# Two-way attention and a squared-ReLU layer on one core: transposes moved from TensorE to DMA, a new order at the start, two column softmaxes moved to the end

## The chip, the core and the metric

The kernel runs on one core of one Trainium2 chip. Its engines work through queues of their own and meet at semaphores: TensorE (PE; its weight loads are listed as PEld), VectorE (DVE), ScalarE (ACT), GpSimd (POOL) and SyncE (SP, which only issues DMAs here). Sixteen DMA engines move data for all of them. TensorE writes to PSUM, eight banks of 2 KB in each of 128 partitions; VectorE and ScalarE copy from there to SBUF. The metric is the device time of one execution in microseconds, as the median of several runs.

## The reference

There are 8 batches of 8 heads, each with a sequence x of 512 rows and a state of 32 rows, both 64 wide. Attention goes both ways over the same scores, and all 4352 rows of the result go through a two-layer network (512 to 2048 to 512):

```python
scores = scale * x @ state.T                    # 512 x 32 per head
xread  = softmax(scores, over the 32) @ state
sread  = softmax(scores.T, over the 512) @ x    # 32 x 512
X = concat(xread, sread), heads side by side    # (8 * 544) x 512
out = (s * relu(X @ w_in) ** 2 + b) @ w_out
```

## The kernel before

Matmuls are in fp16 with fp32 sums. For the 512 x-rows of a batch `X @ w_in` is never formed with xread: the kernel makes M = state @ w_in for each head (8 heads x 32 state rows = two groups of 128 rows, by 2048 columns), and the first layer is A @ M, where A is the first softmax. The names, with lines of the profile:

- **stT**: the transposed state, 64 rows of a head on 64 partitions. `turn_states` makes eight TensorE transposes of the cast states (line 84 through 78), `build_stT` eight ScalarE copies (line 175).
- **xT**: transposed x. `at_x` does 16 TensorE transposes of 128x128 (tile `xps`) and two ScalarE copies of 1024 columns a batch (line 205).
- **T**: the scores, 8 matmuls of 512 columns on 64x32 tiles of the array (`at_T`, line 215), into two banks.
- **First softmax, over 32**: VectorE transposes T in 32x32 blocks (U, 225), takes a maximum per block (mu, 229) and subtracts it (Dm, 235); ScalarE takes the exponential (E1, 242); VectorE sums (z and rz, 249 and 250), multiplies (At, 254) and transposes back (A, 261).
- **Second softmax, over 512 (column softmax)**: VectorE takes the maximum of T (nm, nms: 267, 273), ScalarE the exponential with its sum (E2, 278), VectorE multiplies by the reciprocal (q, a2: 285, 287). `at_aps` transposes a2 with 8 TensorE transposes and one ScalarE copy (a2T, 296), `at_V` multiplies by x with 32 small matmuls (tile `vps`), and VectorE copies the result to srdT (315).
- **M**: four units of 512 columns a batch, each of 8 matmuls (tile `mps`) and two ScalarE copies (330).
- **First layer**: for each f of 16, two matmuls of 512 columns (tile `hps`, 338), an eviction with ReLU on ScalarE to r (340) and a square on VectorE to g (345). **Second layer**: 16 output units a batch of 4 matmuls (tile `ops`, 361), four of them to one block of 128 rows, which VectorE scales and shifts (osb, 371) and SP stores.

The order of the work is written out by hand: what is called first stands first in each engine's queue. A `phase` is sixteen steps. In phase n step f is the first layer of batch n, f, and one unit of the second layer of batch n-1. Lists of (step, piece) hang the other pieces in: in phase n the scores and softmaxes of batch n+1, its a2T and V, and four units of M. Phase 0 and phase 1 have lists of their own, since the start is behind; the last phase, `sr`, runs the first layer of all 256 state rows beside the second layer of batch 7, and the second layer of the state rows follows as a tail.

```python
for b in range(1, B):
    before = []
    if b + 2 < B:
        before += plan_xread(b + 2, (0, 1, 2, 3, 4, 5, 5, 6, 7, 9, 10, 11))
        before += plan_sread(b + 2, (7, 8, 11))
```

SP loads all states (one DMA of 512 KB) and x of batch 0 in fp32 (four of 256 KB), and ScalarE and VectorE cast them. GpSimd's queue loads with a cast to fp16, in this order: w_in 0, x 1, w_in 1 to 3, w_out 0 to 3, x 2; the later x when a buffer is free. One x is four DMAs, in runs of 64 elements.

PSUM is shared out in pairs of banks: `ps_t` for T; `ps_a` (two single banks) for transposes, V and M; `ps_h` for the first layer; `ps_o` for the second.

Of the kernel before, what the change touches and what calls it, by code (L numbers as in the profile page):

```python
# [10 lines left out]
FP32 = mybir.dt.float32  # L11
# [4 lines left out]
def kernel(  # L16
# [11 lines left out]

# [9 lines left out]
    P = 128  # L41
# [6 lines left out]
    ST = S + Ns  # L48
    scale = float(1.0 / np.sqrt(D))
# [3 lines left out]
    konst = ctx.enter_context(tc.tile_pool(name="konst", bufs=1))  # L53
    wpool = ctx.enter_context(tc.tile_pool(name="wpool", bufs=1))
    stage = ctx.enter_context(tc.tile_pool(name="stage", bufs=1))
# [8 lines left out]
    ps_a = ctx.enter_context(tc.tile_pool(name="ps_a", bufs=2, space=bass.MemoryType.PSUM))  # L64
# [4 lines left out]
    def bank(shape, dtype, name, pool=None, tag="pa"):  # L69

        full = (pool or ps_a).tile([P, 2048 // mybir.dt.size(dtype)], dtype, name=name, tag=tag)
        names = " ".join("abc"[: len(shape) - 1])
        sizes = dict(zip("abc", shape[1:]))
        return full[:, 0 : int(np.prod(shape[1:]))].rearrange(f"p ({names}) -> p {names}", **sizes)
# [8 lines left out]
    def transp(out, in_, identity):  # L83
        return mm(out, in_, identity, tp=(0, 0), is_transpose=True)

    RP = B * H * Ns // P
    ident16 = konst.tile([P, P], FP16, name="ident16")
    ident_dr = nc.inline_tensor(np.eye(P, dtype=np.float16), name="ident_const")  # L90
    xf = stage.tile([P, H, SCH, D], FP32, name="xf")
    stf = stage.tile([P, RP, D], FP32, name="stf")
    stn = konst.tile([P, RP, D], FP16, name="stn")
    s_bc = konst.tile([P, 1], FP32, name="s_bc")
    b_bc = konst.tile([P, 1], FP32, name="b_bc")
    ones16 = konst.tile([P, P], FP16, name="ones16")
    bias_bc = konst.tile([P, DM], FP32, name="bias_bc")
    srdT = konst.tile([P, NK, Ns, B], FP16, name="srdT")
    stT = konst.tile([P, B * NK, Ns], FP16, name="stT")
    w_in16 = [wpool.tile([P, NK, 512], FP16, name=f"w_in16_{j}") for j in range(NJ)]  # L100
    w_out16 = [wpool.tile([P, 4, DM], FP16, name=f"w_out16_{q}") for q in range(NKF // 4)]
    xn_t = {}

    def new_xn(b):
        xn_t[b] = xpool.tile([P, SCH, H, D], FP16, name=f"xn_{b}", tag="xn")
        return xn_t[b]

    def load_x(b, c):
        xn = new_xn(b) if c == 0 else xn_t[b]
        nc.gpsimd.dma_start(out=xn[:, c], in_=x[b].rearrange("h (q c) d -> c q h d", q=P)[c])  # L110
# [6 lines left out]
    def load_w_out(q):  # L117
# [4 lines left out]
    nc.sync.dma_start(  # L122
        stf,
        state.rearrange("b h n d -> (b h n) d").rearrange("(p r) d -> p r d", r=RP),
    )
    nc.scalar.dma_start(ident16, ident_dr.ap())
    for k in range(NK):
        nc.sync.dma_start(
            xf[:, 2 * k : 2 * k + 2].rearrange("q h c d -> q h (c d)"),
            x[0, 2 * k : 2 * k + 2].rearrange("h (q c) d -> q h (c d)", q=P),  # L130
        )
# [3 lines left out]
    nc.vector.tensor_copy(stn[:, : RP // 2], stf[:, : RP // 2])  # L135
    nc.gpsimd.tensor_copy(stn[:, RP // 2 :], stf[:, RP // 2 :])
    load_w_in(0)
    for c in range(SCH):
        load_x(1, c)
    for j in range(1, NJ):  # L140
        load_w_in(j)
    for q in range(NKF // 4):
        load_w_out(q)
    for c in range(SCH):
        load_x(2, c)
# [8 lines left out]


# [4 lines left out]
    def heads():  # L160
        for hp in range(4):
            for g in range(NG):
                h = 4 * g + (hp ^ g)
                yield h // 2, h % 2, g, hp

    def build_stT(sl, copies):
        if "sps" not in at[0]:
            turn_states()  # L170
        src = at[0]["sps"].rearrange("p r (bk m u) -> p m bk u r", m=2, u=2)
        dst = stT.rearrange("p bk (u r o) -> p o bk u r", u=2, o=2)
        for m in range(2):
            for o in range(2):
                copies[m](dst[D * m : D * m + D, o, sl], src[D * o : D * o + D, m, sl])

    def turn_states():
        sps = at[0]["sps"] = bank([P, RP // 2, P], FP16, "sps", ps_h, "ph")
        for r in range(0, RP, 2):
            transp(sps[:, r // 2, :], stn[:, r : r + 2, :], ident16)  # L180
# [4 lines left out]
    def sm(b, key, shape, dtype, pool=None, bufs=None):  # L185
        t = (pool or smpool).tile(shape, dtype, name=f"{key}_{b}", tag=key, bufs=bufs)
        at[b][key] = t
        return t

    def blocks(t):  # L190
        return t.rearrange("p g (j n) -> p (g j) n", n=32)

    def over_n(t):
        return t.unsqueeze(2).to_broadcast([P, t.shape[1], 32])

    def at_x(b, kk, copy, n=2):

        if kk == 0:
            sm(b, "xT", [P, NK, S], FP16, apool)
        xps = bank([P, n, S], FP16, f"xps_{b}_{kk}")  # L200
        for k in range(n):
            for c in range(SCH):
                h = 2 * (n * kk + k)
                transp(xps[:, k, P * c : P * c + P], xn_t[b][:, c, h : h + 2, :], ident16)
        copy(at[b]["xT"][:, n * kk : n * kk + n, :], xps)  # L205

    def at_T(b):
        if b:
            T = at[b]["T"] = ps_t.tile([P, NG, S], FP32, name=f"T_{b}", tag="pt")
        else:  # L210
            T = [bank([P, S], FP32, f"T_{b}_{g}", ps_o, "po") for g in range(NG)]
        Tg = at[b]["Tg"] = [T[:, g, :] if b else T[g] for g in range(NG)]
        xT = at[b]["xT"]
        for k, m, g, hp in heads():
            mm(
                Tg[g][Ns * hp : Ns * hp + Ns, :],
                stT[D * m : D * m + D, NK * b + k, :],
                xT[D * m : D * m + D, k, :],
                tp=(D * m, Ns * hp),
            )  # L220


    def at_U(b, g):
        U = sm(b, "U", [P, NG, S], FP32) if g == 0 else at[b]["U"]
        nc.vector.transpose(U[:, g, :], at[b]["Tg"][g])  # L225

    def at_mu(b, g0, g1):
        mu = sm(b, "mu", [P, NG * NSB], FP32) if g0 == 0 else at[b]["mu"]
        nc.vector.tensor_reduce(  # L229
            mu[:, NSB * g0 : NSB * g1], blocks(at[b]["U"][:, g0:g1, :]), AX.X, ALU.max  # L230
        )

    def at_D(b, g0, g1, eng):
        Dm = sm(b, "Dm", [P, NG, S], FP32) if g0 == 0 else at[b]["Dm"]
        eng.tensor_tensor(  # L235
            blocks(Dm[:, g0:g1, :]), blocks(at[b]["U"][:, g0:g1, :]),
            over_n(at[b]["mu"][:, NSB * g0 : NSB * g1]), ALU.subtract,
        )

    def at_E1(b, g0, g1):  # L240
        E1 = sm(b, "E1", [P, NG, S], FP16) if g0 == 0 else at[b]["E1"]
        nc.scalar.activation(E1[:, g0:g1, :], at[b]["Dm"][:, g0:g1, :], AF.Exp, scale=scale)

    def at_z(b, g0, g1):

        z = sm(b, "z", [P, NG * NSB], FP32) if g0 == 0 else at[b]["z"]
        rz = sm(b, "rz", [P, NG * NSB], FP32) if g0 == 0 else at[b]["rz"]
        sl = slice(NSB * g0, NSB * g1)
        nc.vector.tensor_reduce(z[:, sl], blocks(at[b]["E1"][:, g0:g1, :]), AX.X, ALU.add)
        nc.vector.reciprocal(rz[:, sl], z[:, sl])  # L250

    def at_At(b, g0, g1, eng):
        At = sm(b, "At", [P, NG, S], FP16) if g0 == 0 else at[b]["At"]
        eng.tensor_tensor(  # L254
            blocks(At[:, g0:g1, :]), blocks(at[b]["E1"][:, g0:g1, :]),
            over_n(at[b]["rz"][:, NSB * g0 : NSB * g1]), ALU.mult,
        )

    def at_A(b, g0, g1):
        A = sm(b, "A", [P, NG, S], FP16, apool, 3) if g0 == 0 else at[b]["A"]  # L260
        nc.vector.transpose(A[:, g0:g1, :], at[b]["At"][:, g0:g1, :])  # L261


    def at_nm(b):
        nm, nms = sm(b, "nm", [P, NG], FP32), sm(b, "nms", [P, NG], FP32)
        if b:
            nc.vector.tensor_reduce(nm, at[b]["T"], AX.X, ALU.max, negate=True)
        else:
            for g in range(NG):
                nc.vector.tensor_reduce(  # L270
                    nm[:, g : g + 1], at[b]["Tg"][g], AX.X, ALU.max, negate=True
                )
        nc.vector.tensor_scalar(nms, nm, scale, None, ALU.mult)  # L273

    def at_E2(b):
        E2, rs = sm(b, "E2", [P, NG, S], FP16), sm(b, "rs", [P, NG], FP32)
        for g in range(NG):
            nc.scalar.activation(  # L278
                E2[:, g, :], at[b]["Tg"][g], AF.Exp,
                bias=at[b]["nms"][:, g : g + 1], scale=scale, accum_out=rs[:, g : g + 1],  # L280
            )
# [8 lines left out]

    def at_aps(b):
        aps = bank([P, SCH, NG, P], FP16, f"aps_{b}")
        for g in range(NG):
            for c in range(SCH):
                transp(aps[:, c, g, :], at[b]["a2"][:, g, P * c : P * c + P], ident16)
        nc.scalar.copy(sm(b, "a2T", [P, SCH, NG, P], FP16, apool), aps)
# [16 lines left out]

    def at_srd(b):
        nc.vector.tensor_copy(srdT[:, :, :, b], at[b]["vps"])


    def at_M(b, j, pool=None, tag="pa"):
        if j == 0:
# [269 lines left out]
```

## Time and profile before

| | before |
|---|---|
| median of 3 runs | 249.57 us (249.25 to 249.7) |
| span of the profiled execution | 247.4 us |
| time of that execution beside its span | not given apart; the median lies 2.17 us above the span |
| mean granted TensorE clock | 0.993 |
| busy: PE, PEld, DVE, ACT, POOL | 224.2, 105.9, 160.2, 157.5, 31.7 us |
| ops (512 matmuls), hps (256) | 131.7, 78.0 us |
| xps (128 transposes), aps (64) | 11.9, 4.9 us |
| mps (256), T (64), vps (256) | 14.3, 4.9, 5.6 us |
| ACT: r, M, xT, a2T | 76.5, 34.4, 15.2, 8.1 us |

The spans of matmuls overlap, since they are pipelined: what one group costs is the distance from its start to the start of the next. In the chain of work that ended last TensorE has 81% of the span, VectorE 11%, ScalarE 4%. In a line of the order of time the two numbers in front are the start and the length in microseconds; the bracket at its end is the idle time before it and what ended it. Phases begin, by the first xps of a batch, at 42.15 (phase 1), 68.56 (phase 2) and 167.76 (phase 6); phase 7 ends at 214.62, with the first matmul of `sr`, and the tail begins at 235.58.

### The profile page before, as it was taken

Reading aid. Unit: us, or ns where it says so; the run is one execution under the profiler, and the core shown is the slowest. Engines: PE = TensorE matmul, PEld = TensorE weight load, DVE = VectorE, ACT = ScalarE, POOL = GpSimd, SP = SyncE. Lnnn points to the kernel's source line nnn. Section 1 sums busy time; section 2 is a strip of 40 time slices with the busy share of each in tenths; the row PEclk is TensorE's granted clock in tenths of the full one; section 3 lists DMA queues with packets and bytes.
Section 4 is the critical chain, followed back from the end, with each engine's and each line's share of the span. In section 5 each row is a group of like instructions: output and inputs, shape, how many; then the busy total and the mean of one; then the engine's idle time right before and its main releaser. Section 6 shows DMA issues by size and latency. Waiting matters only on the chain.

```text
span 247.4 us, 4277 instructions
## 1 busy us (share of the span) xinstructions
PE 224.2 (91%) x1673; PEld 105.9 (43%) x1673; DVE 160.2 (65%) x306; ACT 157.5 (64%) x284; POOL 31.7 (13%) x41
## 2 busy tenths in 40 slices
PE   1549499968999999999999999999999999999993
PEld 1222134534444444444544444444444444555652
DVE  0499965598659955995599549954996344433330
ACT  2766976768778757875787578757875655433200
POOL 3963100055040050005000000000000000000000
PEclk9999889999999999999999999999999999999999
DMA  5999990299592194119511111111111111121113
GB/s 169 198 186 206 207 143 2 80 75 75 73 117 56 42 107 65 42 46 103 69 44 42 45 42 42 45 42 46 42 42 45 42 42 42 45 86 42 45 45 84
DMA packets 40068, 18.66 MB, mean 75 GB/s; under 512 B 30320, under 2 KB 35696, under 8 KB 40048
## 3 DMA queue, kind: packets, MB, share of 16 engines
q0 software_dynamic: 33344, 7.87, 33.8%
q1 hardware_dynamic: 6272, 10.49, 11.9%
q8 instruction: 13, 0.21, 0.4%
q10 hardware_dynamic: 432, 0.03, 0.1%
q14 instruction: 7, 0.06, 0.1%
HBM read 17.34 MB, written 8.91 MB: 106 GB/s over the span
## 4 chain that ended last, share of the span: by engine, by line
PE 81%; DVE 11%; ACT 4%; DMA 2%; issue 1%; ACTq 0%
PE ops L361 43%; PE hps L338 21%; PE mps L78 4%; PE xps L78 3%; PE hps_sr L338 3%; PE vps L78 2%; DVE U L225 2%; DVE mu L229 2%; DMA stf<-in_state_dram 2%; PE ops_sr L551 1%; PE ops_sr L361 1%; PE aps L78 1%; PE T L78 1%; ACT r L340 1%; DVE g L345 1%; DVE A L261 1%
## 5 line engine op out<-in xcount | busy, mean ns | idle before, releaser
L361 PE MATMUL ops<-w_out,g 128*128 128x512 f16 x512 | 131.7, 380 | 0.0
L340 ACT ACTIVATE r<-hps 128x512 f16<-128x512 f32 x128 | 76.5, 606 | 34.5 <-PE hps L338 33.8
L345 DVE TENSOR_TENSOR g<-r 128x512 f16<-128x512 f16 x128 | 54.5, 431 | 50.7 <-ACT r L340 50.5
L338 PE MATMUL hps<-A,M 128*128 128x512 f16 x256 | 78.0, 389 | 3.9 <-ACT r L340 3.8
L361 PEld LDWEIGHTS <-g 128*128 128x128 f16 x512 | 50.3, 98 | 57.8 <-issue 0.8
L330 ACT CAST M<-mps 128x512 f16<-128x512 f32 x64 | 34.4, 594 | 11.1 <-PE mps L78 10.2
L338 PEld LDWEIGHTS <-M 128*128 128x128 f16 x256 | 21.2, 99 | 31.1 <-issue 16.5
L110 POOL DMA_DIRECT2D xn<-in_x_dram x28 | 24.6, 895 | 77.2 <-PE vps L78 47.1
L371 DVE SCALAR_TENSOR_TENSOR osb<-ops,s_bc,bias_bc 128x512 f32<-128x512 f32 x32 | 23.9, 746 | 0.6 <-PE ops L361 0.6
L205 ACT COPY xT<-xps 128x1024 f16<-128x1024 f16 (+1 forms) x16 | 15.2, 959 | 8.2 <-PE xps L78 8.2
L78 PEld LDWEIGHTS <-xn 128*64 128x64 f16 (+1 forms) x384 | 14.5, 110 | 13.6 <-issue 4.6
L78 PE MATMUL mps<-w_in,stT 64*32 64x512 f16 x256 | 14.3, 399 | 2.9 <-DMA w_in<-in_moe_w_in_dram 1.6
L78 PE MATMUL xps<-ident,xn 128*128 128x128 f16 x128 | 11.9, 241 | 4.3 <-ACT xn L461 2.4
L340 ACT ACTIVATE r_sr<-hps_sr 128x256 f16<-128x256 f32 x16 | 6.1, 383 | 14.5 <-PE hps_sr L338 14.5
L345 DVE TENSOR_TENSOR g_sr<-r_sr 128x256 f16<-128x256 f16 x16 | 4.7, 292 | 12.4 <-ACT r_sr L340 12.1
L78 PEld LDWEIGHTS <-stT 64*32 64x32 f16 x320 | 4.5, 89 | 18.7 <-issue 18.6
L278 ACT ACTIVATE E<-T,nms 128x512 f16<-128x512 f32 x16 | 10.8, 688 | 1.1 <-DVE nms L273 1.1
L225 DVE STREAM_TRANSPOSE U<-T 128x512 f32<-128x512 f32 x16 | 10.5, 692 | 0.7 <-PE T L78 0.7
L261 DVE STREAM_TRANSPOSE A<-At 128x1024 f16<-128x1024 f16 (+1 forms) x9 | 10.1, 1120 | 0.1
L235 DVE TENSOR_TENSOR Dm<-U,mu 128x1024 f32<-128x1024 f32 (+1 forms) x9 | 9.9, 1100 | 0.1
L254 DVE TENSOR_TENSOR At<-E,rz 128x1024 f16<-128x1024 f16 (+1 forms) x9 | 9.9, 1096 | 0.1
L229 DVE TENSOR_REDUCE mu<-U 128x32 f32<-128x1024 f32 (+1 forms) x9 | 9.8, 1094 | 0.1
(44 smaller groups left out, 126.2 us busy)
## 6 DMA issues: line engine op xcount, KB each, us to landing
out_dram<-osb SPq DMA_DIRECT2D x32, 256.0 KB, 2.2
xn<-in_x_dram POOLq DMA_DIRECT2D x28, 128.0 KB, 5.3
w_in<-in_moe_w_in_dram POOLq DMA_DIRECT2D x4, 512.0 KB, 10.5
w_out<-in_moe_w_out_dram POOLq DMA_DIRECT2D x4, 512.0 KB, 15.7
xf<-in_x_dram SPq DMA_DIRECT2D x4, 256.0 KB, 5.8
stf<-in_state_dram SPq DMA_DIRECT2D x1, 512.0 KB, 3.7
out_dram<-osb_sr SPq DMA_DIRECT2D x1, 256.0 KB, 3.0
out_dram<-osb_sr SPq DMA_DIRECT2D x2, 128.0 KB, 2.3
```

Source lines behind the costliest of these rows:

```text
L78: return nc.tensor.matmul(out, lhsT, rhs, start=start, stop=stop, tile_position=tp, is_transpose=is_transpose, skip_group_check=skip,)
L110: nc.gpsimd.dma_start(out=xn[:, c], in_=x[b].rearrange("h (q c) d -> c q h d", q=P)[c])
L205: copy(at[b]["xT"][:, n * kk : n * kk + n, :], xps)
L225: nc.vector.transpose(U[:, g, :], at[b]["Tg"][g])
L229: nc.vector.tensor_reduce(mu[:, NSB * g0 : NSB * g1], blocks(at[b]["U"][:, g0:g1, :]), AX.X, ALU.max)
L261: nc.vector.transpose(A[:, g0:g1, :], at[b]["At"][:, g0:g1, :])
L330: nc.scalar.copy(at[b]["M"][:, g, 512 * j : 512 * j + 512], mps[g])
L338: nc.tensor.matmul(hps, lhsT, rhs, start=(i == 0), stop=(i == len(terms) - 1))
L340: nc.scalar.activation(r, hps, AF.Relu)
L345: nc.vector.tensor_mul(gt, r, r)
L361: nc.tensor.matmul(ops_t[tag, rr], G_t[tag][f][:, P * rr : P * rr + P], w_out_f(f), start=(f == 0), stop=(f == NKF - 1),)
L371: nc.vector.scalar_tensor_tensor(osb, ops_t.pop((tag, rr)), s_bc, bias_bc, ALU.mult, ALU.add)
```

## The change

- Three kinds of transpose go from TensorE and a copying engine to DMA transposes on SP's queue: states of batches 1 to 7 (`turn_states_dma`, 14 blocks of 128x128), x of batches 1 to 7 (`at_x_dma`, 16 blocks each) and a2 of all batches (in `at_a2`, 8 blocks). `at_aps`, `build_stT` and most uses of `at_x` go.
- States are loaded as rows (r p), two blocks first, and are cast twice side by side, so that a transposed block has each state on both halves of the partitions. A transposed block of x holds two neighbouring rows, one on each half of the partitions, so T's two banks are the two row parities p, with both head groups g in each: 16 matmuls of 256 columns.
- x of batch 0 is also loaded with a cast by GpSimd, first in its queue, in two halves; one x is one DMA (runs of 256 elements). The order is x 0, w_in 0, w_in 1, x 1, w_in 2, w_in 3, the casts of the states, w_out 0 to 3, x 2, x 3, x 4.
- The first softmax of batch 0 and the first layer's f 0 to 7 are done in halves (row parity p, head group g). Nine matmuls that compute nothing (`idle`) stand between them.
- M is made in pairs of units, one in `ps_a`, which is now one buffer of two banks, and one in `ps_t` (`own`); its copies hang in the four steps that follow.
- The column softmaxes of batches 0 and 1 are done in phase 7 (`late`), with their scores computed again; V of the others is one phase later.

```diff
-    nc.sync.dma_start(
-        stf,
-        state.rearrange("b h n d -> (b h n) d").rearrange("(p r) d -> p r d", r=RP),
-    )
+    state_rows = state.rearrange("b h n d -> (b h n) d").rearrange("(r p) d -> p r d", p=P)
+    nc.sync.dma_start(stf0[:, 0:2], state_rows[:, 0:2])
     nc.scalar.dma_start(ident16, ident_dr.ap())
-    for k in range(NK):
-        nc.sync.dma_start(
-            xf[:, 2 * k : 2 * k + 2].rearrange("q h c d -> q h (c d)"),
-            x[0, 2 * k : 2 * k + 2].rearrange("h (q c) d -> q h (c d)", q=P),
-        )
+    load_x(0, 2)
...
+    nc.sync.dma_start(stf1, state_rows[:, 2:])
     load_w_in(0)
-    for c in range(SCH):
-        load_x(1, c)
-    for j in range(1, NJ):
-        load_w_in(j)
+    load_w_in(1)
+    load_x(1)
+    load_w_in(2)
+    load_w_in(3)
+    for u in range(2):
+        nc.gpsimd.tensor_copy(stn[:, 2:, u], stf1)
     for q in range(NKF // 4):
         load_w_out(q)
-    for c in range(SCH):
-        load_x(2, c)
+    load_x(2)
...
+    def turn_states_dma(r0, r1):
+        nc.sync.dma_start_transpose(
+            stT[:, r0:r1], stn[:, r0:r1].rearrange("p r u d -> p (r u d)")
+        )
...
+    def at_x_dma(b):
+        new_xT(b)
+        nc.sync.dma_start_transpose(
+            at[b]["xT"], xn_t[b].rearrange("q h c d -> q (h c d)")
+        )
...
     def at_a2(b):
...
+        nc.sync.dma_start_transpose(
+            sm(b, "a2T", [P, NG * SCH, P], FP16, apool), a2.rearrange("p g s -> p (g s)")
+        )
...
+    def idle(n):
+        dps = ps_o.tile([P, DM], FP32, name=f"dps_{nc.next_id()}", tag="po")
+        for _ in range(n):
+            nc.tensor.matmul(dps, ones16[:, :P], ones16, start=True, stop=True)
...
+    turn_states(0, 2, act)
+    at_x(0, 0, (dve, act))
+    at_T(0, (0,))
+    idle(2)
+    for p in range(2):
+        at_U(0, p, 0)
+    at_mu(0, g=0)
+    at_D(0, g=0)
+    at_x(0, 1, (act, act))
+    at_T(0, (1,))
+    idle(1)
+    at_E1(0, g=0)
+    at_U(0, 0, 1)
...
+    at_M2(0, 0)
+    idle(4)
+    at_M2(0, 1)
+    idle(2)
+    turn_states_dma(2, RP)
+    at_x_dma(1)
+    at_x_dma(2)
...
+    for f in range(8):
+        layer1_x(0, f, 1)
+        square(0, f, 1)
+    at_M2(0, 2)
+    at_T(1)
+    for f in range(8, 12):
+        layer1_x(0, f)
...
+    at_M2(0, 3)
+    layer2(0, 0, 0)
...
+    at_M2(1, 0)
+    for q in (1, 2):
+        for rr in range(2):
+            layer2(0, rr, q)
+        at_M2(1, q, q == 2)
+    bias_sum()
+    for rr in range(2):
+        layer2(0, rr, 3)
+    bias_all()
+    for rr in range(2):
+        out_x(0, rr)
...
+    def late(b, s):
+        return [
+            (s[0], lambda: at_T(b)),
+            (s[1], lambda: at_nm(b)),
+            (s[2], lambda: at_E2(b, (0,))),
+            (s[3], lambda: at_E2(b, (1,))),
+            (s[4], lambda: at_a2(b)),
+            (s[5], lambda: at_V(b)),
+        ]
...
+    for b in range(0, B):
+        before, behind = [], l2(b) if b else first
+        behind = left + behind
+        if b + 3 < B:
+            before += [(0, lambda b=b: load_x(b + 3)), (9, lambda b=b: at_x_dma(b + 3))]
+        if b + 2 < B:
+            s = (0, 1, 2, 3, 4, 4, 5, 7, 8, 10, 11) if b else (4, 5, 6, 7, 8, 8, 9, 11, 12, 13, 15)
+            before += chain(b + 2, s)
+            before += [(13 if b else 15, lambda b=b: at_a2(b + 2))]
+        if b and b + 1 < B:
+            before += [(4, lambda b=b: at_V(b + 1))]
+        one = [(b + 1, 3), (b + 2, 0)][: B - 1 - b]
+        two = [(b + 2, 1), (b + 2, 2)] if b + 2 < B else []
+        make, copies, _ = pieces(7 if b else 9, 1, *one)
+        before, behind = before + make, behind + copies
+        make, copies, left = pieces(12 if b else 14, 0, *two)
+        before, behind = before + make, behind + copies
+        if b == B - 2:
+            before += late(0, (0, 1, 2, 3, 4, 11)) + late(1, (6, 7, 8, 9, 10, 14))
         phase(b + 1 if b + 1 < B else "sr", before, behind)
```

In `chain` the eleven steps are those of T, U, nm, E2 of each group, mu, Dm, E1, z, At and A.

## The prediction

> **What bounds the kernel now.** I read the page first (slices of the span, groups, DMA issues), then the busy time of stages cut where a batch's phase begins, then the order of time in the two stages that differ. The page says that TensorE is full from about 37 us to the end, and not before:
>
> ```profile
> PE   1549499968999999999999999999999999999993
> ...
> PEclk9999889999999999999999999999999999999999
> ```
>
> In the stages below (busy time by engine, granted clock, DMA share, GB/s; from 68.56 four whole phases) the steady phases are TensorE alone: 99.20 of 99.20 us, 24.80 each, with VectorE at 73.93 / 4 = 18.5 and ScalarE at 18.3. Phase 1 (42.15 to 68.56) is not: TensorE works 22.66 of 26.41.
>
> ```profile
> core 0: us, PE busy (x) PEld busy (x) DVE busy (x) ACT busy (x) POOL busy (x), PEclk, DMA share, GB/s
> ...
> 42.15:68.56 26.41, 22.66 (x242) 11.16 (x241) 19.47 (x39) 19.18 (x33) 7.96 (x10) 1.00 0.71 71
> 68.56:167.76 99.20, 99.20 (x770) 45.59 (x769) 73.93 (x137) 73.06 (x128) 9.58 (x11) 1.00 0.37 59
> 192.56:214.62 22.06, 22.06 (x122) 9.49 (x121) 9.45 (x21) 12.49 (x22) 0.00 (x0) 1.00 0.13 48
> ```
>
> TensorE in order of time (start, length, what): what a group takes is the distance to the next group, less 0.43 for two hps or 0.86 for four ops. Eight transposes take 0.44 (68.56 to 69.00). T and a unit of M back to back take 0.56; a unit alone 0.34; with the 0.09 of drain in front of each, 0.65 and 0.43.
>
> ```profile
> 68.56 0.61 PE L78 MATMUL xps<-ident,xn 128*128 128x128 f16 x8
> 69.00 0.59 PE L338 MATMUL hps<-A,M 128*128 128x512 f16 x2
> ...
> 72.13 0.41 PE L78 MATMUL T<-xT,stT 64*32 64x512 f16 x8
> 72.36 0.40 PE L78 MATMUL mps<-w_in,stT 64*32 64x512 f16 x8
> 72.69 0.61 PE L338 MATMUL hps<-A,M 128*128 128x512 f16 x2
> ...
> 76.68 0.41 PE L78 MATMUL mps<-w_in,stT 64*32 64x512 f16 x8
> 77.02 0.61 PE L338 MATMUL hps<-A,M 128*128 128x512 f16 x2
> ```
>
> At the start a chain sets the time: state, x, T at 10.57, softmax, first layer at 20.44. Beside it the cast loads run without a break until 36. GpSimd's waits for a landed w_in end at 19.52, 22.05 and 24.60, so a 512 KB slab lands every 2.55 us.
>
> ```profile
> 10.57 1.20 PE L78 MATMUL T<-xT,stT 64*32 64x512 f16 x8
> ...
> 20.44 3.81 PE L338 MATMUL hps<-A,M 128*128 128x512 f16 x10
> ...
> 24.60 0.87 POOL L110 DMA_DIRECT2D xn<-in_x_dram  x1 [1.67 <-DMA w_in<-in_moe_w_in_dram]
> ```
>
> The span is 247.4 us; no time of that execution is given beside it, so the sum goes against the median, 249.57, which holds 2.17 us around the span. I carry those unchanged.
>
> **Part 1, the steady phases 2 to 6.** Each loses 16 transposes of x and 8 of a2: 3 x 0.44 = 1.32 us of TensorE. M in pairs: today T + M (0.65) and three units alone (1.29) make 1.94; afterwards T (0.43) and two pairs (1.30) make 1.73, 0.21 less. T becomes 16 matmuls of 256 columns, the same columns: between 0 and 0.2 more (32 small vps matmuls issue in 0.64, 20 ns each, so 8 more cost at most 0.16). Net 1.3 to 1.5, taken 1.4: five phases, **-7.0**. Is all of it on the path? TensorE is busy throughout, and the next are VectorE (18.5, unchanged but for the form of nm and U) and ScalarE, which loses two xT copies and one a2T copy (1.01 each): 15.3. Both lie below 23.4. Four M copies now come on four steps with E1: 4 x (0.61 + 0.59) + 1.06 = 5.9 us against 4 steps of 1.29 and a pair of M, 5.8; two hps buffers cover that, and if not, a few tenths a phase.
>
> **Part 2, the DMA transposes.** Sixteen of them (one of 14 state blocks of 128x128, seven of 16 x blocks, eight of 8 a2 blocks) go on SP's queue, which after the first loads carries only stores today. No trace shows one. By rows:
>
> ```profile
> xn<-in_x_dram POOLq DMA_DIRECT2D x28, 128.0 KB, 5.3
> ...
> stf<-in_state_dram SPq DMA_DIRECT2D x1, 512.0 KB, 3.7
> ```
>
> Cheap end: 512 KB on the same queue, 3.7 us (stf); 256 KB stores land in 2.2. Dear end: the x loads in 256-byte pieces, 128 KB in 5.3 us, so 21.2 for the 512 KB of one x and 10.6 for an a2. I take 4 for x and 2.5 for a2, nearest to stf: the same queue and bytes, whole partitions. In a steady phase x is issued in step 9 and used in step 0 of the next, 7 steps or some 10 us later; a2 in step 13, used in step 4. Both are covered while x takes under about 10 us. They add waits: x 2's transpose holds SP until x 2 has landed near 37, with no store behind it before 40; a2's holds it for VectorE's two multiplications (0.7), with the phase's last store behind it; the stores have four osb buffers, a whole phase's worth, so neither costs. TensorE's T and V wait in order, and everything of TensorE stands behind them: that is where a late transpose would be paid. POOL goes from 28 x loads to 9, in 1 KB pieces; its 24.6 us of issue were hidden and nothing is gained there.
>
> **Part 3, the start, to the beginning of phase 2 (68.56 today).** The first state rows are 64 KB, x 0 comes as 512 KB in halves: first T near 6.3 against 10.57 (the x half reads 512 KB as stf does, 3.7 after an issue at 0.9; then 8 transposes and a copy, 1.03 + 0.6 in today's rows). Softmax of the first half: U 2 x 0.36, mu 0.69, Dm 0.69, the same for 256 more of the second group 1.1, E1 0.4, z 0.66 + 0.25, At 0.69, A 0.71, with the second x half between: 13.5. M 0 and 1 need w_in 1: slabs from 5.6 (x 0) at 2.55 each, and 2.2 for the other state rows, give 12; ScalarE has copied by 14.6. The second half's A follows near 18.2, first layer by 21.4 (16 evictions of 0.38). The nine idle matmuls (0.43 cold) lie in these waits; if the weights came early, four would delay M by 1.7. T of batch 1 needs GpSimd's state casts (2 x 1.5, after 9), their transpose and that of x 1, near 20 to 21: beside the path, by little. From 21.4 TensorE has 3.5 of hps, 1.7 of M, 6.9 of ops and 1.0 of cps, but w_out 3 lands only at 34 to 35.5 (eleven slabs and 1 MB of transposes at 2.55 per 512 KB). Then cps tail, 8 ops (1.73) and bias: phase 1 begins near 38.5, against 42.15, with one M unit and 8 ops more done.
> Phase 1 holds no x, a2T or V: TensorE 13.8 + T 0.43 + two pairs 1.3 = 15.5. It is VectorE's: x 2 lands at 37, its transpose at 42 to 43 (x 3 and x 4 load beside it), T at 43. Behind T stand U 1.38, nm 1.39, mu 1.21, Dm 1.22, ten squares 4.3, osb 0.75, z 1.56, At 1.21, A 1.24, a wait of 1.2 for E1: 15.5, and A of batch 2 is there at 59. So phase 2 begins at 59 instead of 68.56: **-9.6**. Two units of M are done ahead; three V are still owed.
>
> **Part 4, phase 7 and the end.** Phase 7 gains two T (0.86) and three V (3 x 0.64), loses two M units (0.86): **+1.9**. V of batch 1, in step 14, waits for an a2 whose E2 is in steps 8 and 9: 0 to 1 us, left in the range. The sr phase and the tail (32.8) stay.
> Sum: -7.0 - 9.6 + 1.9 = -14.7; 249.57 - 14.7 = **235** (234.9).
>
> A row that could take some of part 3 back: 24 to 36 us today has TensorE busy 8.77 of 12 and a granted clock of 0.86 (PEclk 8 in two slices); the hps at 29.88 take 1.87 for four, 0.47 each against 0.22, about 2.6 us over twelve matmuls. [...] It costs nothing while the weights set the pace, so my sum leaves it to the range.
>
> **Rivals.**
> *Transposes dear (ends slower).* At the dear end one phase needs 21.2 + 10.6 = 31.8 us of SP's queue against 23.4: five phases +42; the start has state (18.5), x 1, x 2 in a row from 12: x 2 at 73, A at 89, phase 2 thirty later than forecast: 235 + 72 = 307. It decides from 11.5 us per x: T of batch 2 then comes at 12 + 1.875 x 11.5 = 33.6, x 2 at 37 + 11.5 = 48.5 (6 later), and each steady phase waits 1.5 to 2 us (+8 to 9): all gain gone. Against it: nothing in the rows but stf and the stores; for it: the small-piece loads. [...]
> *The start gives little.* Transposes share the engines with loads (DMA share 1.5 from 12 to 36), so T 1, w_out 3 and x 2 slip by 4 to 9 us, each in front of an in-order TensorE: phase 2 at 63 to 68, total 239 to 244; 241 in the middle.
> *Steady phases do not shrink.* ScalarE's and VectorE's bunched steps hold them at 24.8: 235 + 7 = 242. For it: 5.9 against 5.8 above; against it: both engines under 19 in the sum.
>
> **How the numbers follow.** Forecast 0.56 (its own range 231 to 239), start gives little 0.18, no shrinking 0.10, transposes dear 0.14; 0.02 for a sum of losses that lands within 0.2% (0.5 us, about what can be told from no change). Faster 0.84, same 0.02, slower 0.14. The range, 230 to 246, leaves out the slower cases and a tail of the first.
>
> **What would show it.** Phase distance 23.4 (23.1 to 23.8) between first hps of successive batches; first hps near 14, phase 2 near 59, phase 7 near 24; SP's transposes landing in 3 to 5 us for x; no wait of T for xT after batch 2. Wrong if T waits for xT in each phase, if the relu of VectorE's late squares holds hps, or if w_out lands after 38.

## The result: slower, 258.75 us

The changed kernel takes 258.75 us (median of 4 runs, 258.57 to 259.38) against 249.41 us (249.13 to 249.7), a ratio of 1.0375 with a 95% interval of 1.0357 to 1.0393. The forecast was 235. The profiled execution took 258.57 us, with a span of 256.8. The slices of its page (each 6.4 us) say where:

```profile
PE   0796000499888999999999999999999999999993
...
PEclk9999655599999999999999999999999999999999
DMA  4999999940214476318814841183013132512113
```

Before, TensorE was never idle for a whole slice behind the first; now three slices hold nothing, with the granted clock down to half, while the DMA engines are full. TensorE in order of time shows the hole, and that it is one wait:

```profile
24.75 0.41 PE L74 MATMUL mps<-w_in,stT 64*32 64x512 f16 x8
48.50 0.63 PE L74 MATMUL T<-xT,stT 64*32 64x256 f16 x16 [23.34 <-DMA xT<-xn]
49.07 3.16 PE L358 MATMUL hps_None<-A,M 128*128 128x512 f16 x8
```

T of batch 1 waits 23.34 us for the transposed x of batch 1, and all of TensorE stands behind it. The chain that ended last, up to that T (start, length, what), tells what it waited for:

```profile
4.08 15.57 DMA stf<-in_state_dram
...
19.70 2.39 POOL stn L144 x2
...
22.10 6.08 SPq L175
...
28.23 20.23 DMA xT<-xn
```

The 448 KB of the other states take 15.57 us to land, the casts 2.4, and the two transposes, in one queue, 26.4 us from 22.10 to 48.46. The DMA issues (count, median us to landing) show that this is a matter of the start alone:

```profile
a2T<-a SPq DMA_TRANSPOSE x8, 3.0
xT<-xn SPq DMA_TRANSPOSE x7, 4.7
...
stT<-stn SPq DMA_TRANSPOSE x1, 17.2
```

The median transpose of an x takes 4.7 us and that of an a2 3.0. Behind the hole the kernel does what was forecast. By stages (busy time by engine, granted clock, DMA share, GB/s): the idle wait, the first matmuls behind it, phase 1, two of the steady phases, phase 7, and the end.

```profile
25.10:48.50 23.40, 0.06 (x8) 0.10 (x1) 0.29 (x1) 1.21 (x3) 2.53 (x3) 0.55 1.31 174
48.50:52.10 3.60, 3.56 (x24) 1.08 (x23) 2.83 (x3) 1.66 (x3) 0.00 (x0) 0.62 1.37 185
64.53:84.05 19.52, 16.32 (x114) 6.56 (x113) 16.73 (x30) 13.88 (x27) 0.00 (x0) 1.00 0.27 68
84.05:107.28 23.23, 23.23 (x177) 10.10 (x176) 18.97 (x37) 16.29 (x31) 0.88 (x1) 1.00 0.62 114
107.28:130.51 23.23, 23.23 (x177) 10.10 (x176) 18.42 (x34) 15.65 (x30) 0.88 (x1) 1.00 0.51 103
200.21:224.10 23.89, 23.89 (x232) 11.12 (x232) 14.69 (x33) 13.07 (x27) 0.00 (x0) 1.00 0.34 68
224.10:256.80 32.70, 28.38 (x179) 17.23 (x176) 10.46 (x25) 6.38 (x17) 0.00 (x0) 0.99 0.17 57
```

A steady phase takes 23.23 us with TensorE full (24.80 before). Phase 2 begins at 84.05, against 68.56 before and 59 in the forecast.

### The profile page after: what moved, and what is told of

Its sections match the earlier page's. It is cut to its first block, busy times and chain, and to the rows that moved or that the text cites. A ratio compares the mean times of both kernels' runs of the same rounds, so it can differ in the third digit from the quotient of the medians.

```text
span 256.8 us, 4168 instructions
## 1 busy us (share of the span) xinstructions
PE 215.2 (84%) x1612; PEld 97.7 (38%) x1612; DVE 160.2 (62%) x307; ACT 135.1 (53%) x264; POOL 16.3 (6%) x23
## 4 chain that ended last, share of the span: by engine, by line
PE 73%; DMA 14%; ACT 4%; SPq 2%; DVE 2%; issue 1%; POOL 1%; ACTq 1%
PE ops L385 41%; PE hps_None L358 20%; DMA xT<-xn 8%; DMA stf<-in_state_dram 6%; PE mps L74 3%; PE hps_sr_None L358 3%; SPq L175 2%; PE vps L74 2%; ACT M L340 1%; PE ops_sr L604 1%; PE T L74 1%; PE ops_sr L385 1%; ACT r_None L360 1%; POOL stn L144 1%; ACT E L262 1%
## 5 line engine op out<-in xcount | busy, mean ns | idle before, releaser
L360 ACT ACTIVATE r_None<-hps_None 128x512 f16<-128x512 f32 x120 | 71.3, 598 | 80.3 <-PE hps_None L358 74.3
L358 PE MATMUL hps_None<-A,M 128*128 128x512 f16 x240 | 71.3, 386 | 1.1 <-ACT r_None L360 0.9
L367 DVE TENSOR_TENSOR g<-r_None 128x512 f16<-128x512 f16 x120 | 49.9, 427 | 23.4 <-ACT r_None L360 22.0
L358 PEld LDWEIGHTS <-M 128*128 128x128 f16 x272 | 24.2, 99 | 36.1 <-issue 12.6
L245 DVE STREAM_TRANSPOSE U<-T 128x1024 f32<-128x1024 f32 (+1 forms) x11 | 10.4, 950 | 27.0 <-PE T L74 26.9
L395 DVE SCALAR_TENSOR_TENSOR osb<-ops,s_bc,bias_bc 128x512 f32<-128x512 f32 x32 | 23.7, 743 | 0.7 <-PE ops L385 0.6
L74 PEld LDWEIGHTS <-stT 64*32 64x32 f16 x416 | 4.7, 90 | 39.6 <-issue 25.1
L112 POOL DMA_DIRECT2D xn<-in_x_dram x9 | 7.9, 884 | 108.5 <-PE vps L74 107.8
L267 DVE TENSOR_REDUCE z<-E 128x32 f32<-128x1024 f16 (+1 forms) x9 | 9.9, 1101 | 7.5 <-ACT E L262 7.4
L360 ACT ACTIVATE r_sr_None<-hps_sr_None 128x256 f16<-128x256 f32 x16 | 6.1, 384 | 14.4 <-PE hps_sr_None L358 14.4
L255 DVE TENSOR_TENSOR Dm<-U,mu 128x1024 f32<-128x1024 f32 (+2 forms) x10 | 10.1, 1006 | 0.1
L322 DVE CAST srdT<-vps 128x128 f16<-128x128 f32 x8 | 5.8, 728 | 6.9 <-PE vps L74 6.9
L249 DVE TENSOR_REDUCE mu<-U 128x32 f32<-128x1024 f32 (+2 forms) x10 | 10.0, 997 | 0.1
## 6 DMA issues: line engine op xcount, KB each, us to landing
w_out<-in_moe_w_out_dram POOLq DMA_DIRECT2D x4, 512.0 KB, 12.6
stf<-in_state_dram SPq DMA_DIRECT2D x1, 448.0 KB, 15.6
```

The lines of the kernel that those rows point to most:

```text
L74: return nc.tensor.matmul(out, lhsT, rhs, start=start, stop=stop, tile_position=tp, is_transpose=is_transpose, skip_group_check=skip,)
L245: nc.vector.transpose(part(U, p, g), part(at[b]["T"], p, g))
L249: nc.vector.tensor_reduce(part(mu, p, g), blk(part(at[b]["U"], p, g)), AX.X, ALU.max)
L255: nc.vector.tensor_tensor(blk(part(Dm, p, g)), blk(part(at[b]["U"], p, g)), over_n(part(at[b]["mu"], p, g)), ALU.subtract,)
L358: nc.tensor.matmul(hps, lhsT, rhs, start=(i == 0), stop=(i == len(terms) - 1))
L360: nc.scalar.activation(r, hps, AF.Relu)
```

## The experiments

The theory after this reading: a DMA transpose, and a load in 256-byte pieces, are cheap by themselves and several times dearer beside the cast loads of w_in, w_out and x, and the wait of T for them is the whole loss. All experiments start from the changed kernel; those with a ratio were timed in three rounds against the kernel before, the others have one time. "turn_states" and "at_x" are the TensorE transposes that batch 0 uses anyway.

### The two transposes of the start given back to TensorE

```diff
-    turn_states_dma(2, RP)
-    at_x_dma(1)
     at_x_dma(2)
...
     at_M2(0, 2)
+    turn_states(2, 10, act)
+    turn_states(10, RP, dve)
+    at_x(1, 0, (dve, act))
+    at_x(1, 1, (dve, act))
     at_T(1)
```

> States of batches 1 to 7 and x of batch 1 are turned by TensorE again, in front of T of batch 1; all else is as in the changed kernel, and the rest of the states still lands late. Theory (the loss is the two DMA transposes at the start, which crawl beside the cast loads): T of batch 1 near 27.5 instead of 48.5, no wait of 23 us, phase 2 begins near 63 and the time is 235 to 241. Rival (the loss lies in the new order as such: halves, pairs of M, late softmaxes): the wait moves elsewhere and the time stays above 250.

Measured: 239.2 us (238.37 to 240.69), ratio 0.9583 (0.9531 to 0.9635). T of batch 1 starts at 28.44, phase 2 at 63.72, the steady phases take 23.25. What follows: these two transposes alone turn a gain of 4% into a loss of 4%. The other fourteen stay on the DMA queue in this kernel, and no matmul waits for any of them.

### One of the two given back

```diff
-    at_x_dma(1)
...
     at_M2(0, 2)
+    at_x(1, 0, (dve, act))
+    at_x(1, 1, (dve, act))
     at_T(1)
```

> x 1 is turned by TensorE, the rest of the states still by the DMA transpose. Theory (each DMA transpose crawls beside the cast loads by itself): the state transpose is asked for near 22.1 and lands after 15 to 17 us as in the changed kernel, near 38 to 39.3; T of batch 1 waits some 10 us for it and starts near 39.5 instead of 48.5, and the time is 258.6 less 9, 248 to 251. Rival (they crawl because the two share one queue and one set of engines): alone it takes about 6 us as with the loads held, T starts near 29, and the time is 239 to 241.

and the other way round:

```diff
-    turn_states_dma(2, RP)
...
     at_M2(0, 2)
+    turn_states(2, 10, act)
+    turn_states(10, RP, dve)
     at_T(1)
```

> The rest of the states are turned by TensorE, x 1 still by the DMA transpose, which now need not wait behind the state transpose on SP's queue. Theory (each crawls by itself): asked for when x 1 has landed, near 15 to 20, it takes 17 to 20 us beside w_out's loads, so T of batch 1 starts at 32 to 40 instead of 28.4, and the time is 239 plus 4 to 11, 243 to 250. Rival (only the two together crawl): it lands within 5 to 8 us, before TensorE comes to T near 28, and the time is 238 to 240.

TensorE in order of time, first with only the states turned by DMA, then with only x 1:

```profile
39.33 0.63 PE L74 MATMUL T<-xT,stT 64*32 64x256 f16 x16 [11.82 <-DMA stT<-stn]
```

```profile
31.50 0.63 PE L74 MATMUL T<-xT,stT 64*32 64x256 f16 x16 [5.46 <-DMA xT<-xn]
```

Measured: 250.01 and 242.25 us. The states' transpose takes 17.2 us again without the other in its queue; so each is slow by itself, and the rival falls. But x 1's, issued at 19.84, is there at 31.5, after 11.6 us and not the 17 to 20 expected, and T and the time come out just under the theory's ranges: of the 20.23 us of the changed kernel more than half were a place in the queue. Its own share there is the 9.2 us from 39.3 (where the states' transpose lands) to 48.5.

The kernels with nothing else changed lie on one line, T of batch 1 against the time of the profiled execution:

| turned by DMA at the start | T of batch 1 at | time |
|---|---|---|
| states and x 1 (the change) | 48.50 | 258.57 |
| states | 39.33 | 250.01 |
| x 1 | 31.50 | 242.25 |
| neither | 28.44 | 238.37 |

From first to last that is 20.2 us in 20.1: a microsecond of T is a microsecond of the kernel.

### The states asked for earlier

```diff
+    stf1 = stage.tile([P, RP - 2, D], FP32, name="stf1", tag="stf")
     nc.sync.dma_start(stf0[:, 0:2], state_rows[:, 0:2])
+    nc.sync.dma_start(stf1, state_rows[:, 2:])
```

(stf0 has a buffer of its own, so the second DMA need not wait for its casts.)

> The remaining 14 blocks of state rows get a buffer of their own and are asked for at 1.2 us, ahead of the cast loads, instead of 4.1. Both DMA transposes stay. Theory (transposes crawl beside cast loads): the rows land near 5 instead of 19.7, the state transpose starts near 9 and still takes 15 us or more, x 1's ends at 35 to 38; time 246 to 250. Rival (only lateness: a transpose takes 4 to 5 us whenever it starts): T of batch 1 waits for nothing, time 235 to 239.

Measured: 250.66 us, just above the theory's range. The load lands in 7.4 us instead of 15.6, and the transpose of the states starts at 10.53 instead of 22.10; but it then takes 15.2 us, T still waits 12.9 for x 1 and starts at 40.04, and x 0 lands in 8.0 us instead of 6.0. So the late start is part of the loss, and not the cause of the slow transposes.

### The states in larger pieces

```diff
-    nc.sync.dma_start(stf1, state_rows[:, 2:])
+    nc.sync.dma_start(
+        stf1,
+        state.rearrange("b h n d -> (b h n) d")[2 * P :].rearrange("(p r) d -> p r d", p=P),
+    )
```

> The changed kernel, but the remaining 448 KB of state rows are read as one run of 3.5 KB per partition instead of fourteen runs of 256 bytes (batches 1 to 7 so get the rows of other heads: the output is not the reference's). Asked for at 4.1 us as before. Theory (the engines take turns by piece, so small pieces get little of them beside the cast loads): they land within 4 to 8 us instead of 15.6, the state transpose starts near 13 instead of 22 and still crawls; time 249 to 254. Rival (engines share by bytes, or the queue waits for the casts whatever the pieces): 13 to 16 us again, time 257 to 260.

A partition now reads one run of 3.5 KB instead of fourteen of 256 bytes, and the rows of the states fill other places. Measured: 253.01 us. The load lands in 8.1 us instead of 15.6, in 144 packets of SP's queue instead of 1808 (packets between its issue and its landing). The transpose behind it takes 17.9 us, T starts at 42.90. So the size of the pieces set the load's price; the transposes keep theirs.

### The loads held back

```diff
-    for q in range(NKF // 4):
-        load_w_out(q)
-    load_x(2)
...
     turn_states_dma(2, RP)
     at_x_dma(1)
+    gate = konst.tile([P, 2], FP16, name="gate")
+    nc.gpsimd.tensor_copy(gate, at[1]["xT"][:, 15, 0:2])
+    for q in range(NKF // 4):
+        load_w_out(q)
+    load_x(2)
     at_x_dma(2)
```

> GpSimd asks for w_out 0 to 3 and x 2 and later only after x 1 has been turned (a copy of two elements of the turned x 1 stands in front of them). Theory (contention): from 22 us on only the tail of w_in 3 runs beside the transposes; the states take 4 to 7 us instead of 17.2 and x 1 5 to 8 instead of 20.2, T of batch 1 at 30 to 34; w_out 3 lands near 45, time 241 to 247. Rival (these two are slow of themselves, as the first on the queue or by their form): 17 and 20 us again, T of batch 1 at 48, weights later, time above 260.

The DMA issues of this kernel:

```profile
xT<-xn SPq DMA_TRANSPOSE x7, 4.6
...
stT<-stn SPq DMA_TRANSPOSE x1, 6.5
```

Measured: 247.61 us, just above the theory's range. With the loads out of the way the states' transpose takes 6.5 us instead of 17.2, x 1's 5.8 (issued at 24.67), and T of batch 1 starts at 30.47. The loads that come later cost elsewhere: T of batch 2, at 48.6 with TensorE's transposes, now starts at 55.87 and waits 3.40 for x 2. Holding loads back is no remedy; it shows the cause.

### Loads put beside the steady transposes

```diff
+        if b in (2, 3):
+            before += [(1, load_junk)]
```

(load_junk loads six 512 KB slabs of w_in, with the cast to fp16, to tiles that nothing reads.)

> The changed kernel with six cast loads of 512 KB that nobody reads in each of phases 3 and 4 (behind the loads of x 5 and x 6 on GpSimd's queue), beside the transposes of x 5 and x 6; phases 2, 5 and 6 are left as they are. Theory (contention with cast loads): those two transposes land in 10 to 18 us instead of 4.3 to 4.7, the others as before; time 258.7 to 268. Rival (the start is special): all land within 6 us and the time stays at 258.7.

TensorE in order of time:

```profile
118.44 0.63 PE L74 MATMUL T<-xT,stT 64*32 64x256 f16 x16 [10.49 <-DMA xT<-xn]
...
152.94 0.63 PE L74 MATMUL T<-xT,stT 64*32 64x256 f16 x16 [9.42 <-DMA xT<-xn]
```

Measured: 282.61 us. The two x transposes beside the added loads land in 19.5 and 18.5 us, the a2 transposes in 12.7 and 12.9, and behind the start T waits in just those two phases. The cheap transposes of the steady phases are made four times as dear by the added cast loads alone. Both the landing and the time lie above the theory's ranges (18 us, 268). The two waits are 19.9 of the 24.0 us by which this kernel is slower than the changed one, and behind each wait TensorE runs at half pace for a while (granted clock 0.50 from 118.44 to 122). No run put loads without a cast there.

### Smaller packets in the loads

What the two queues share was the last question. The DMA queues of the changed kernel between 22.1 and 39.3 us, while the states' transpose was on its way (packets, MB, time of the packets as a share of 16 engines; q0 has GpSimd's cast loads, q1 SP's DMAs):

```profile
q0 software_dynamic: 2460, 2.43, 94.3%
q1 hardware_dynamic: 1920, 0.48, 32.0%
```

The loads move 988 bytes a packet, the transposes 250; over this stretch the queues get 1.3 to 1 by packets and 5 to 1 by bytes. From 32 to 36 us, where both had work all the time, the packets are equal:

```profile
q0 software_dynamic: 625, 0.62, 91.4%
q1 hardware_dynamic: 626, 0.16, 30.0%
```

So w_out was loaded in runs of a quarter of the length:

```diff
-        nc.gpsimd.dma_start(
-            w_out16[q], moe_w_out.rearrange("(q f p) n -> q p f n", p=P, f=4)[q]
-        )
+        for c in range(4):
+            nc.gpsimd.dma_start(
+                w_out16[q][:, :, P * c : P * c + P],
...
```

> w_out is loaded in sixteen transfers with runs of 128 columns (256 bytes in SBUF) instead of four with runs of 512 (1 KB); the bytes are the same, and so is all else. Theory (the two queues share the DMA engines packet for packet, as the 2460 to 1920 packets between 22.1 and 39.3 us of the changed kernel suggest, and the transposes move 256 bytes in a packet): the transpose of the states now passes small packets instead of large ones and lands 8 to 12 us after its issue instead of 17.2, with bytes of both queues within a factor of 1.5; T of batch 1 starts at 38 to 44 instead of 48.5, and the time is 248 to 255. Rival (the cast loads take their share by bytes, or the transposes are slow of themselves beside any load): the state transpose still takes 15 to 19 us, T starts at 47 to 52, and the time is 257 to 263.

The states' transpose in the DMA issues of this kernel, and its queues between 24 and 28 us, while nearly all of that transpose passed:

```profile
stT<-stn SPq DMA_TRANSPOSE x1, 9.6
```

```profile
q1 hardware_dynamic: 1768, 0.45, 82.5%
q0 software_dynamic: 749, 0.22, 69.5%
```

Measured: 249.49 us, T at 38.51, both in the theory's ranges, and the states' transpose takes 9.6 us instead of 17.2. But this transpose does not test the theory. Its 448 KB are 1792 packets of 256 bytes, and 1768 packets of its queue moved in these 4 us, against 749 of the loads. It met a lull in the loads (0.22 MB in 4 us; in the changed kernel 0.62 MB from 32 to 36), and why the loads came thin just there is not shown.

The transpose of x 1 behind it does test it. Here are the queues beside it, first in this kernel between 32 and 37 us, then in the changed kernel between 41 and 45, where the loads of x ran:

```profile
q0 software_dynamic: 1678, 0.42, 82.0%
q1 hardware_dynamic: 1679, 0.43, 65.1%
```

```profile
q0 software_dynamic: 966, 0.49, 87.8%
q1 hardware_dynamic: 963, 0.25, 46.5%
```

In each of these three stretches both queues get the same number of packets, whatever the loads carry in one: 156 a microsecond each beside loads of 990 bytes a packet, 241 beside 510, 336 beside 250. So while both had work there they shared by packets, one to one, and in the changed kernel the transposes lose because their packets are the small ones, 256 bytes against 990 and 510.

### Nearly all transposes given back

```diff
+    def at_x_te(b):
...
+    def at_aps(b):
...
-            before += [(0, lambda b=b: load_x(b + 3)), (9, lambda b=b: at_x_dma(b + 3))]
+            before += [(0, lambda b=b: load_x(b + 3)), (9, lambda b=b: at_x_te(b + 3))]
...
-            before += [(4, lambda b=b: at_V(b + 1))]
+            before += [(2, lambda b=b: at_aps(b + 1)), (4, lambda b=b: at_V(b + 1))]
```

(on top of the first experiment; x 3 to 7 and a2 2 to 7 by TensorE into two banks, ScalarE copies. x 2 and a2 0 and 1 stay with the DMA.)

> As the kernel with states and x 1 turned by TensorE, and also x 3 to 7 (16 transposes and two ScalarE copies each, in step 9) and a2 of batches 2 to 7 (8 transposes and a copy, in step 2) turned by TensorE; only x 2 and the two late a2 stay with DMA. Theory (the steady gain is the TensorE time of the transposes): 5 x 0.88 + 6 x 0.44 = 7.0 us more than the 239.2 without, 245 to 247.5. Rival (the gain comes from the start, the pairs of M and the late softmaxes; ScalarE or VectorE hold the phases): within 2 us of 239.2.

One phase of this kernel, from a pair of M to the next (columns as above), and its transposes of an x in TensorE's order of time:

```profile
86.14:111.39 25.25, 24.89 (x200) 11.50 (x201) 18.41 (x34) 18.10 (x33) 0.87 (x1) 1.00 0.30 63
```

```profile
106.36 1.05 PE L74 MATMUL xps<-ident,xn 128*128 128x128 f16 x16 [0.36 <-ACT M L363]
```

Measured: 251.84 us (250.7 to 252.03), ratio 1.0083 (1.0056 to 1.0111), 12.6 more than the first experiment, not 7.0. A phase takes 25.25 instead of 23.25, and phase 2 begins at 66.27 instead of 63.72: 5 x 2.0 + 2.55 = 12.6. Of the 2.0, 16 and 8 transposes take 0.89 + 0.45, a wait for a copy of M that holds the banks 0.36; where the other 0.3 goes is not shown. So in the steady phases, and against this placement, the DMA transposes are worth more than TensorE's own time for them.

### Without the idle matmuls

```diff
-        for _ in range(n):
+        for _ in range(0):
             nc.tensor.matmul(dps
```

(on top of the first experiment)

> As the kernel with states and x 1 turned by TensorE, without the nine idle matmuls. Theory of the prediction (they lie in waits, and what they hold up is the clock): matmuls from 17 to 30 us start at half the rate, ScalarE covers most of that; 239 to 241.5. Rival (they only take time): 237.5 to 239.

TensorE where the idle matmuls stood:

```profile
15.88 0.63 PE L74 MATMUL mps<-w_in,stT 64*32 64x512 f16 x8 [2.80 <-DMA w_in<-in_moe_w_in_dram]
```

The first-layer matmuls between 17 and 20 us (count, busy time, mean ns of one, idle time before them), first without the idle matmuls, then in the first experiment:

```profile
L358 PE MATMUL hps<-A,M 128*128 128x256 f16 x12 | 3.0, 403 | 0.5 <-DVE A L279 0.3 <-ACT r L360 0.2
```

```profile
L358 PE MATMUL hps<-A,M 128*128 128x256 f16 x14 | 2.3, 270 | 0.9 <-ACT r L360 0.6 <-DVE A L279 0.2
```

Measured: 238.26 us (238.03 to 239.04), ratio 0.9554 (0.9532 to 0.9576); T of batch 1 at 28.37 and phase 2 at 63.66, as in the first experiment to 0.1. The expected loss did not come, though its cause did: without the idle matmuls one of these takes 403 ns, with them 270, as after 22.4 us in both. (The granted clock reads 1.00 in this stretch in both, so the profile's clock does not show it.) What the faster matmuls gain is spent on waits for ScalarE's evictions, and the M unit behind the first layer's f 0 to 7 starts at 24.66 without the idle matmuls and at 24.73 with them. So they lie in waits, as the prediction had it; they raise the pace, and here no time hangs on it. This is the lowest median of the kernels, but its range overlaps that of the first experiment.

### First-layer work between TensorE's transposes

```diff
+    turn_states(2, 10, dve)
+    for f in range(8, 10):
+        layer1_x(0, f)
+    turn_states(10, RP, dve)
+    at_x(1, 0, (dve, dve))
+    for f in range(10, 12):
+        layer1_x(0, f)
+    at_x(1, 1, (dve, dve))
     at_T(1)
-    for f in range(8, 12):
-        layer1_x(0, f)
```

(in place of the turns of the first experiment)

> As the kernel with states and x 1 turned by TensorE, but f 8 to 11 of the first layer stand between these transposes, ahead of T of batch 1, and VectorE makes the copies, so that ScalarE's evictions and the transposes run side by side. If the stretch from 25 to 32 us is on the path: 1.5 to 2.5 us less, 236.5 to 238. Rival (phase 1's softmax sets the time, or squares stand behind the copies on VectorE): 239.

Measured: 239.15 us (239.03 to 240.11), ratio 0.9597 (0.957 to 0.9624): no gain over the first experiment, where 1.5 to 2.5 us were expected; what sets the time of that stretch is not shown.

## Why the prediction was wrong

**What bounds the kernel, and Part 1: right.** (The page's line has TensorE at 6 and 8 tenths from 49.5 to 61.8 us, so it is not full from 37 on; the sum did not use that, and the row of phase 1 beside it has it right.) A steady phase was to take 23.4 us and takes 23.23; over five, 0.8 us less than forecast. VectorE and ScalarE stay below TensorE (18.4 and 15.7 of 23.23), so the rival in which the steady phases do not shrink fell.

**Part 2, the price of a DMA transpose: this step failed.** It took one price, 4 us for an x, "nearest to stf: the same queue and bytes, whole partitions". The row it leaned on, 512 KB in 3.7 us, was timed in the first 4.5 us of the kernel before, where GpSimd's queue moves no packet yet. For the steady phases the price was good (4.7 and 3.0 against 4 and 2.5). For the start it was not: 17.2 us for the states and another 9.2 for x 1 against 4 each. The dear end of the range came nearer for the states (18.5 by the small-piece loads), but by luck: 20 of those 28 loads ran after 42 us, beside little but stores, and were no test of a transpose beside weights. What was missed is that a price belongs to the stage in which it was timed.

No one price for an x holds throughout. The median of a kernel is 4.3 to 4.7 us from issue to landing; with nothing beside it, x 1 of the kernel with the loads held back moved its packets within 2 us (2082 from 28 to 30); the two beside added loads took 19.5 and 18.5. It depends on what the DMA engines do beside.

**Part 3, the start: the size followed from that step and from one more term.** T of batch 1 was to be ready "near 20 to 21: beside the path, by little". The forecast gave the load of the other state rows 2.2 us and had the states cast from 9 on, to 12; they landed at 19.65 (again a DMA in small packets beside the loads), 10.6 late; the casts took 0.6 less than the 3.0 reckoned; the transposes took 26.4 instead of 8, 18.4 more. That makes 48.5 out of 20. The prediction itself put 1 MB of transposes into the loads' sum, at the loads' rate of 2.55 us per 512 KB, which is a share by bytes; the trace shows shares by packets (625 and 626 from 32 to 36 us). One of its signs of being wrong came too: w_out's last slab landed at 40.7, after 38, but no matmul waited for it, since TensorE stood still until 48.5.

The difference of 23.7 us between 258.57 and 234.9, by the prediction's terms:

| term | forecast | measured | difference |
|---|---|---|---|
| end of the work ahead of T of batch 1 | 21.4 | 25.1 | +3.7 |
| wait for T of batch 1 | 0 | 23.4 | +23.4 |
| from there to phase 1 (64.53) | 17.1 | 16.0 | -1.1 |
| phase 1 | 20.5 | 19.5 | -1.0 |
| phases 2 to 6 | 117.0 | 116.2 | -0.8 |
| phase 7 | 24.0 | 23.9 | -0.1 |
| tail | 32.8 | 32.7 | -0.1 |
| around the span | 2.2 | 1.8 | -0.4 |

The sum of the last column is 23.6. The first row is a smaller miss of its own (0.35 of it is an M unit that the 21.4 does not hold). It is there at the first hps already, at 17.23 instead of 14: first T came at 7.97 instead of 6.3, x's first half landing at 6.3 instead of 4.6, and w_in 1, put at 12 though its own terms add to 12.9, was waited for until 15.88 in the kernel without idle matmuls. The best kernel, at 238.26, keeps this miss: its phase 2 begins at 63.66 instead of 59. The third row is near by luck: its 17.1 held a wait for w_out, and the 16.0 hold none, but matmuls at half pace.

**Part 4: right.** Phase 7 takes 23.89 (22.06 + 1.9 = 23.96 forecast), the tail 32.70.

**The clock.** The prediction left half-clock matmuls to the range, since they cost nothing where the weights set the pace. Now they stand behind the wait, on the path: eight hps take 3.09 us to the next group's start, about 1.3 more than the 8 x 0.22 of full speed, with a granted clock of 0.62 over 3.6 us. (Its row of the kernel before was priced too high: by the distance to the next group the twelve matmuls from 29.88 take 4.04 us, 1.4 more than at full speed, and not 2.6.) Half pace lasts some 2.7 us here: the granted clock reads 0.50 from 48.50 to 51.20 and 0.96 from there to 52.10. No one length fits all runs: behind a wait of 3.40 us in the kernel with the loads held back the granted clock stays at 0.50 from 55.87 to 61.5.

**The rivals.** "Transposes dear" had the side right and only half the place: the start, not the phases. In the phases, with x at 4.7 us, its condition of 11.5 never came near. (The T that it puts at 33.6 is that of batch 1, not 2.) "The start gives little" had the mechanism, transposes sharing the engines with loads ahead of an in-order TensorE, with 4 to 9 us where it was 25. I had summed two outcomes as if one price governed start and phases together; the true case mixed them.

## What to carry to other kernels

Price a DMA by a row from the stage where it will run, and ask what queue is full there: a price timed in a quiet stage says nothing of a loaded one (an x took 4.7 us in the median and 18.5 to 19.5 beside cast loads). A DMA transpose is a good way to take work from a busy TensorE in a stage with idle DMA engines and some 10 us of slack (2.0 us a phase here, at DMA shares of 0.18 to 0.62), and a bad one in front of an in-order engine while weights stream in (a wait of 23.34 us here). Where a load must pass others, look at its packets: fewer and larger ones came through in half the time (8.1 us against 15.6).

## What was not expected of the hardware

- While two DMA queues on the same engines both had work, they got equal packets: 625 and 626, 966 and 963, 1678 and 1679, with loads of 990, 510 and 250 bytes a packet beside transposes of 256.
- The same 448 KB landed in 15.6 us as runs of 256 bytes and in 8.1 us as runs of 3.5 KB, beside the same loads.
- A DMA transpose of 512 KB took 4.3 to 4.7 us (medians) with no cast load beside it and 18.5 to 19.5 beside cast loads; 256 KB of a2 took 3.0 and 12.7 to 12.9.
- The states' 14 blocks took 17.2 us and x 1's 16 only 9.2 largely since the loads beside them had packets of 990 and of 510 bytes: at 156 and 241 packets a microsecond, 1792 and 2048 packets need 11.5 and 8.5 us. With only x 1 turned by DMA it took 11.6, of which 2 us, from 24 to 26, moved 1777 of its 2048 packets in a lull of the loads (83 packets).
- What else the 17.2 us hold is open: the first 2 us of the states' transpose, in which its queue moved nothing (issued at 22.10, no packet before 24), and two lulls, 26 to 27 and 30 to 31 us, in which neither queue moved much (59 and 74 packets, against some 300 in a full microsecond).
- Matmuls of 256 columns took 403 ns where the profile's granted clock reads 1.00, and 270 behind the idle matmuls. There the profile's clock did not tell the pace, and the length of the matmuls did.
